# Two memory-recurrent attention layers with SwiGLU on one core: another TensorE order, and weight remainders loaded by 128-partition transfers

## The chip, the cores and the metric

One core of one Trainium2 chip runs the whole program. The metric is the device time of one execution in microseconds; the kernel before took 2661.49 us in the median of three runs (2657.86 to 2663.87). The engines are called PE (TensorE; PEld is its weight load), DVE (VectorE), ACT (ScalarE), POOL (GpSimd) and SP (SyncE, which only issues DMAs here).

## What is computed

The sequence has 2048 rows of 576 numbers. Two layers follow each other with the same weights; each is a recurrent attention over 64 segments of 32 rows, with 8 memory rows carried from segment to segment, and then a gated FFN of width 4608:

```python
for s in range(n_seg):                       # 64 segments, one after the other
    h = concat([mem, x[s]])                  # 8 + 32 rows
    q, k, v = h @ Wq, h @ Wk, h @ Wv         # 576 -> 32 heads x 128
    p = softmax(mask(q k^T * scale))         # 40 x 40 for each head
    o = (p @ v) @ Wo
    mem, out[s] = o[:8], o[8:]
# twice: x = x + A(layernorm(x)); x = x + B(layernorm(x))
# B: (silu(x @ w1) * (x @ w3)) @ w2
```

Weights and results are bfloat16.

## The kernel before

**Stages.** The two layers run interleaved: step t computes segment t of the first layer and segment t - 8 of the second (`LAG`), 72 steps in all. In steps 8 to 63 both layers are at work and share every matmul's columns (80 columns, 40 of each). Four steps make 128 rows, and their FFN runs spread over the next steps.

**The order of the work.** `make_nodes` builds a graph of work items with estimated durations (`dur`) and result latencies (`lat`), `plan` places them on the engines by these estimates, and the instructions are emitted in the planned order; each engine then runs its own list in order and waits by semaphores. DVE, ACT, POOL and the DMA list of SP get their order from the plan's estimated times and priorities. TensorE's order is not planned: it is a string of letters, `ORDER = FIRST + FOUR * 11 + LAST` (L222). FIRST covers steps 0 to 15, each FOUR four steps, LAST steps 60 to 71. One letter is one work item; the next item of that kind is taken. The kinds, with the matmuls of one and the mode of TensorE in which they run in FOUR:

- Q, q: queries and keys of four heads, 32 matmuls over the 512 even rows of the weights (full) and 8 over their last 64 rows (row)
- S: scores of a group of eight heads, 16 (col); P: weights times values, 8 or 16 (full or col); O, o: output projection, 32 (full) and 8 (col)
- V, v and G, g: values (V over four column strips, G full or col; v and g the last 64 rows)
- F, f: gate and up projection of 256 FFN columns (F full or col, f row); W, w: down projection of the two layers (full or col)
- n, a, b, p: transpositions of rows around the layer norms

A kind with two modes joins the mode that its neighbours have; when the mode changes, the matmuls in flight have to finish first, and the plan adds 0.1 to 0.14 us (L33, L34).

**The softmax of a group.** Behind S, DVE adds the mask and subtracts the maximum, ACT takes the exponential, DVE sums and writes the normalised probabilities to PB, SP issues a DMA transposition from PB to PTS (L1061), and P reads PTS. There are two buffers of PB and one of PTS (`POOLS`, L38): the transposition of a group waits until the P before it is done. The plan takes 1.27 us for the issue and 2.45 us until the data is there (L402). A step has four groups.

**Weights in the loop.** The FFN weights are read again for every four steps: a unit of 256 columns has four DMAs into one of two W13 buffers (two of the 512 even rows, two of the 64-row remainders) and one into one of two W2C buffers. They are issued by SP, on the same queue as the transpositions. A load waits until the unit before the last has been used up.

**Weights at the start.** Wq, Wk and Wv have 576 rows, four times 128 and a remainder of 64. T.W holds Wq in chunks 0 to 3, Wk in 4 to 7, and in chunk 8 both remainders: Wq's in partitions 0 to 63, Wk's in 64 to 127, all 4096 columns each. T.WV has Wv's remainder likewise: of each group of 1024 columns the first 512 in partitions 0 to 63, the others in 64 to 127. These are loaded by four DMAs of 64 partitions (`load_tails`, L701): SP issues Wq's and half of Wv's first of all, ACT issues Wk's, then x and the memory, then the rest of Wv's. Behind them SP issues sixteen pieces of 512 KB of Wq and Wk (first the left 2048 columns of both, then the right), then Wv, then Wo. `qk_tail` (L957) runs the two remainders of four heads as pairs of matmuls on opposite halves of the rows. At the end of the program chunk 8 and the rest of T.W take FFN weights (`tail_load`), 512 columns at a time, once the last step's q letters have read them.

Of the kernel before, what the change touches and what calls it, by code (L numbers as in the profile page):

```python
# [77 lines left out]
def plan(nodes, pools, letters):  # L78


    for n in nodes:
        for d in n.deps:
            d.outs.append(n)
    kinds = {}
    for n in nodes:
        if n.eng == "PE":
            kinds.setdefault(KINDS[n.name], []).append(n)
    its = {k: iter(v) for k, v in kinds.items()}
    seq = [next(its[c]) for c in letters]
    assert len(seq) == sum(len(v) for v in kinds.values())  # L90
    free = {k: [0.0] * c for k, c in pools.items()}
    t_eng = {e: 0.0 for e in ("PE", "ACT", "DVE", "POOL", "DMA", "SWD")}
    ready = {e: [] for e in t_eng}
    both = []
    mode, run = [], []
    order = []

    def settle():
        for x in run:
            x.mode = mode[0]  # L100
        run.clear()
    at = 0

    def push(n):
        if n.eng != "PE":
            (both if n.eng == "AD" else ready[n.eng]).append(n)

    def est(e, n):
        t = max(t_eng[e], n.ready)
        need = {}  # L110
        for s in n.acq:
            if s.i is None:
                need[s.pool] = need.get(s.pool, 0) + 1
        for p, c in need.items():
            t = max(t, sorted(free[p])[c - 1])
        return t

    for n in nodes:
        if n.left == 0:
            push(n)  # L120
    while len(order) < len(nodes):
        best = None
        for e in t_eng:
            if e == "PE":
                cands = seq[at:at + 1] if at < len(seq) and seq[at].left == 0 else []
            else:
                cands = ready[e] + (both if e in ("ACT", "DVE") else [])
            if not cands:
                continue
            ests = [(est(e, n), n) for n in cands]  # L130
            t = min(x for x, _ in ests)
            if t >= NOW:
                continue
            if best is None or t < best[0]:
                best = (t, e, ests)
        if best is None:
            raise RuntimeError(f"the plan is stuck at {at}: {seq[at].name}")
        t, e, ests = best
        st, n = min((x for x in ests if x[0] <= t + 1e-9), key=lambda x: x[1].prio)
        dur = n.dur  # L140
        if isinstance(dur, tuple):
            dur = dur[0] if e == "ACT" else dur[1]
        if e == "PE":
            at += 1
            if not any(m in mode for m in n.mode):
                dur += SWITCHES.get(f"{mode[0]} {n.mode[0]}", SWITCH) if mode else SWITCH
                settle()
                mode = n.mode
            mode = [m for m in mode if m in n.mode]
            run.append(n)  # L150
        elif n.eng == "AD":
            both.remove(n)
        else:
            ready[e].remove(n)
        n.start, n.end, n.by = st, st + dur, e
        t_eng[e] = n.end
        for s in n.acq:
            if s.i is not None:
                continue
            f = free[s.pool]  # L160
            s.i = min((i for i in range(len(f)) if f[i] <= st + 1e-9), key=lambda i: f[i])
            f[s.i] = NOW
        for s in n.rel:
            s.users -= 1
            s.end = max(s.end, n.end + (PE_LAT if e == "PE" else n.lat if e == "DMA" else EW_LAT))
            if s.users == 0:
                free[s.pool][s.i] = s.end
        for m in n.outs:
            m.ready = max(m.ready, n.end + (0.0 if m.eng == e == "PE" else n.lat))
            m.left -= 1  # L170
            if m.left == 0:
                push(m)
        order.append(n)
    settle()
    return order
# [20 lines left out]
def ewh(*ns):  # L196
# [11 lines left out]
    "oWQqfqqQQQfqSFSVvqqfQQFFPWSfqqQwQFSPaffOwWFPOFOPWOwfooooFfqqQQWQqqSQQqqSbQGgqqSQQgPGSGPGggOPOwOPoooOo"  # L208
)
FOUR = (  # L210
    "QqqqqQppQQVvSSnnQqfFQqfFSQQqfqPFOWoPSwFffOPFOowoWPFOoFfqfQQQQqqqwSWFSGfqgqQQQPQqgqWSSGFPFffggGGPwOOFPOOffWooooFv"
    "VqqqQQQwSFfqqqQQQSwWFSPFfqfqQQOwSPoWFFPffOOwPWOoooFfqqqQQWqSaQQQbSQqgqGSQPQqqgGOSPGggoOPGwOPooOo"
)
LAST = (
    "QqqqpQQQSnpQQqqqVvSnSQfqFFPqfQOWPSwoFffOPFoOFPwOffWooFQQQqqqFQSqffqFQQqgSWGSQPwQqqgfGSFPFgfgGwOPOGOPWOffooooFQQq"
# [16 lines left out]
def make_nodes(em, nseg, pools, o=Opt, dma_bw=230e3, load_bw=345e3):  # L232
# [122 lines left out]
    def step(t):  # L355
# [17 lines left out]
        for g in range(NG):  # L373
# [25 lines left out]
            pbs = node("DVE", w, em.sm_pb(t, g, sme, pb), deps=[d], prio=pf, acq=[pb], rel=[sme], name="pb")  # L399
            pts = Slot("pts")  # L400
            if nl == 2:
                tr = node("DMA", 1.27, em.ptr_dma(t, g, pb, pts), deps=[pbs], prio=pf - 0.02, acq=[pts], name="TR", lat=2.45)  # L402
            else:
                bt = banks()
                tr = node("PE", 8 * mm80, em.ptr(t, g, pb, bt), deps=[pbs], prio=pf + o.tr, mode="full/col", acq=[pts] + bt, name="TR")
# [54 lines left out]
    def job(j):  # L460
# [24 lines left out]
        def units(pps, at0, end):  # L485
            for at, pp in enumerate(pps, at0):
# [3 lines left out]
                for pr_ in (2 * pp, 2 * pp + 1):  # L490
                    prio = (s0 + 4 if end and not last else s0) + o.ff + (o.win if s0 + 4 < nst else o.last_win) * (2 * at + pr_ % 2) / NPR
                    if stays:
                        w13, w2 = kept[pr_]
                        ld = []
                        w2s.append(w2)
                    elif in_tail:
                        w13 = w2 = None
                        ld = tail[pp]
                    else:
                        keep = before_last and pp == npp - 1  # L500
                        w13, w2 = Slot("w13", users=2 + keep), Slot("w2", users=ne + keep)
                        kept[pr_] = w13, w2
                        ld = [node("DMA", kb(1152, 256) / dma_bw, em.load_w13(pr_, w13), prio=prio - 1, acq=[w13], lat=2.8, name="W13")]
                        lds.append(node("DMA", kb(256, 576) / dma_bw, em.load_w2(pr_, w2), prio=prio - 0.99, acq=[w2], lat=2.0, name="W2l"))
                        w2s.append(w2)
                    b = banks()
                    htt = Slot("htt", users=ne)
                    rel13 = [w13] if w13 else []
                    fm = node("PE", 16 * mm, em.ffn_up(ents, pr_, w13, b, in_tail, False), deps=wr + ld, prio=prio, mode="full/col",
                              acq=b + [htt], rel=rel13, name="FF")  # L510
                    ff = node("PE", 2 * mm, em.ffn_up(ents, pr_, w13, b, in_tail, True), deps=wr + ld, prio=prio + o.fft, mode="row",
                              acq=b + [htt], rel=rel13, name="FFt")
                    a = node("ACT", actc(256 * ne), em.ffn_tanh(ents, b, htt), deps=[fm, ff], prio=prio - 0.5, name="tanh")
                    c = node("DVE", 2 * dve(256 * ne) + 0.13, em.ffn_mul(ents, b, htt), deps=[a], prio=prio - 0.5, rel=b, name="mul")
                    last_up[:] = [fm, ff]
                    mids.append(c)
                    htts.append(htt)
# [24 lines left out]
        if last:  # L542
# [3 lines left out]
            for i in range(8):  # L546
                g = gates.get(i)
                tail.append([load("tail", kb(128, c), s0 + o.tail_at + 0.01 * i, em.tail_load(i, what, g), deps=dep + [g])
                             for what, c, dep in ((0, 9 * 512, qk_done[2 * i:2 * i + 2]), (1, 4 * 576, v_done))])
            shared.pop()()  # L550
        norm()
        if last:
# [55 lines left out]
class Emitter:  # L608
# [91 lines left out]

    def load_tails(self, what):  # L701
        def f(n):
            if what < 2:
                d, wd = (self.dma, self.a.wq) if what == 0 else (self.adma, self.a.wk)
                d(self.T.W[what * R64:(what + 1) * R64, 8, :], wd[4 * P:D, :])
            if what != 1:
                r = what // 2
                (self.adma if r else self.dma)(self.wv(True)[r * R64:(r + 1) * R64, :].rearrange("p (q n) -> p q n", q=NG),
                                               self.a.wv[4 * P:D, :].rearrange("p (q r n) -> r p q n", q=NG, r=2)[r])
        return f  # L710

    def wv(self, tail):
# [227 lines left out]
    def qk(self, t, u, b):  # L940
# [13 lines left out]
                                first and j == 0 and c == 0, c == 3)  # L954
        return f

    def qk_tail(self, t, u, b):  # L957
        def f(n):
            q0, q1 = self.qcols(t)
            HTt = self.ht(t)  # L960
            first = self.begin(b)
            for j in range(4):
                h0 = self.head(u // 2, 4 * (u % 2) + j) * E
                for kind in (0, 1):
                    rr = slice(kind * R64, (kind + 1) * R64)
                    self.mm(self.bk(b[kind])[:, j * SW:j * SW + q1 - q0], self.T.W[rr, 8, h0:h0 + E], HTt[rr, 4, q0:q1],
                            first and j == 0, True, tile_position=(kind * R64, 0))
        return f

    def qk_ev(self, t, u, r, q, b):  # L970
# [420 lines left out]
```

## Time and profile before

| what | us |
|---|---|
| three runs, median (lowest, highest) | 2661.49 (2657.86, 2663.87) |
| the profiled execution | 2662.86 |
| its span, from first to last instruction | 2661.1 |
| PE busy in 0 to 56, 56 to 528 | 26.8, 456.8 |
| PE busy in 528 to 2222 (eleven times FOUR) | 1678.4 |
| PE busy in 2222 to 2600, 2600 to 2661 | 369.8, 53.5 |

The loads at the start, by the trace of the DMA issues (issue to landing, us from the start of the span): Wk's remainder 0.7 to 5.5, Wq's 0.7 to 7.9, x 1.3 to 8.4, half of Wv's remainder 1.4 to 9.7 and the other half 2.8 to 13.7; the first 512 KB of Wq 2.3 to 11.5, the eighth piece landed at 21.2, the sixteenth at 34.7, Wv between 37.2 and 44.7, Wo between 47.6 and 56.7.

In a row of the profile, the numbers behind the bar of a group are busy time, mean duration and idle time before; a timeline row has the start, the time taken, the engine, line, operation and tiles, and in brackets the idle time before it with what ended it. A row of the stretches has the stretch, its length, busy time and instructions of PE, PEld, DVE, ACT and POOL, the granted TensorE clock, the busy share of the DMA engines and GB/s. The granted clock over the span is 0.994.

### The profile page before, as it was taken

The numbers are of one execution on the slowest core, as the hardware profiler recorded it, in microseconds if no ns is written. First come the engines' busy times: TensorE is split into PE (matmuls) and PEld (weight loads), VectorE is DVE, ScalarE is ACT, GpSimd is POOL, SyncE is SP. The second block draws the span as 40 slices with busy tenths as digits, with TensorE's granted clock in tenths as the row PEclk, the third lists the DMA queues.
The fourth block names the chain that finished last, engine by engine and source line by source line (L and its number), as shares of the span: only waits on it lengthen the run. The fifth ranks groups of instructions, "written<-read, shape, count | busy, mean of one in ns | idle before, by whom it ended". The sixth has DMA issues, their size and how long they took to land.

```text
span 2661.1 us, 134392 instructions
## 1 busy us (share of the span) xinstructions
PE 2585.4 (97%) x59795; PEld 2228.9 (84%) x59795; DVE 2025.0 (76%) x5276; ACT 1252.0 (47%) x3612; POOL 337.1 (13%) x399
## 2 busy tenths in 40 slices
PE   5999999999999999999999999999999999999998
PEld 4788888888888888888888888888888888888887
DVE  4787777787787778777777777777778777777876
ACT  2555453454445444444544444454544445454453
POOL 1111110110111011011101101110111111011110
PEclk8999999999999999999999999999999999999999
DMA  9064845556565556555554655645465564544457
GB/s 321 4 179 123 189 105 149 127 136 148 128 144 105 147 125 145 142 131 147 113 139 116 162 128 141 154 110 136 113 155 125 143 157 101 129 119 128 128 158 236
DMA packets 688135, 371.55 MB, mean 140 GB/s; under 512 B 234072, under 2 KB 682336, under 8 KB 686912
## 3 DMA queue, kind: packets, MB, share of 16 engines
q1 hardware_dynamic: 684016, 355.07, 53.2%
q8 instruction: 467, 7.65, 1.2%
q0 software_dynamic: 3024, 6.93, 0.9%
q10 hardware_dynamic: 512, 0.94, 0.1%
q14 instruction: 116, 0.95, 0.1%
HBM read 306.72 MB, written 2.36 MB: 116 GB/s over the span
## 4 chain that ended last, share of the span: by engine, by line
PE 67%; DMA 7%; DVE 4%; ACT 1%; SPq 1%; issue 1%; POOL 0%; DVEq 0%; POOLq 0%; ACTq 0%
PE bank L632 67%; DMA PTS<-PB 4%; DMA W<-in_B_w_dram 2%; DVE STAT L638 1%; DMA W2C<-in_B_w_dram 1%; DVE SME L638 1%; SPq L641 1%; DVE PB L638 1%; DVE V L638 1%; ACT V L635 0%; DVE XR L638 0%; DVE HTT L638 0%; DVE QKT L638 0%; POOL PB L1052 0%; ACT QKT L635 0%
## 5 line engine op out<-in xcount | busy, mean ns | idle before, releaser
L632 PEld LDWEIGHTS <-W 128*128 128x128 bf16 (+2 forms) x32576 | 1270.4, 101 | 137.4 <-issue 58.6
L632 PE MATMUL bank<-HT,W 128*128 128x80 bf16 (+3 forms) x23040 | 800.0, 197 | 25.9 <-DMA W<-in_A_Wk_dram 8.5
L632 PE MATMUL bank<-XTB,W 128*64 128x256 bf16 (+5 forms) x9536 | 663.2, 263 | 6.3 <-DMA W<-in_B_w_dram 5.9
L1052 POOL MEMSET PB<- 128x1024 bf16 x288 | 273.9, 951 | 1958.6 <-DMA PTS<-PB 1292.0
L635 ACT ACTIVATE QKT<-bank 128x256 bf16<-128x256 f32 (+4 forms) x1456 | 338.9, 310 | 284.6 <-PE bank L632 272.1
L632 PE MATMUL bank<-OT,WO 128*128 128x80 bf16 (+3 forms) x11520 | 417.3, 198 | 1.5 <-issue 0.8
L632 PEld LDWEIGHTS <-WO 128*128 128x128 bf16 (+1 forms) x11520 | 386.2, 102 | 36.8 <-issue 20.9
L635 ACT ACTIVATE V<-bank 64x512 bf16<-64x512 f32 (+1 forms) x625 | 351.7, 585 | 120.2 <-PE bank L632 112.3
L632 PE MATMUL bank<-WV,HT 128*32 128x512 bf16 (+4 forms) x3688 | 370.2, 384 | 1.3 <-DVE HT L638 0.7
L632 PE MATMUL bank<-W2C,HTT 128*64 128x288 bf16 (+1 forms) x3296 | 321.5, 287 | 4.7 <-DMA W2C<-in_B_w_dram 4.7
L635 ACT ACTIVATE OT<-bank 128x320 bf16<-128x320 f32 (+1 forms) x384 | 144.3, 403 | 335.6 <-PE bank L632 332.1
L638 DVE TENSOR_REDUCE STAT<-SME 104x8 f32<-104x320 f32 (+1 forms) x576 | 274.6, 477 | 32.4 <-ACT SME L635 27.0
L638 DVE TENSOR_TENSOR PB<-SME,STAT 40x128 bf16<-40x128 f32 (+4 forms) x912 | 275.5, 336 | 12.2 <-POOL PB L1052 0.4
L638 DVE SCALAR_TENSOR_TENSOR HTT<-HTT,bank 128x512 bf16<-128x512 bf16 (+1 forms) x324 | 201.2, 621 | 105.0 <-ACT HTT L635 101.9
L632 PEld LDWEIGHTS <-HT 128*32 128x32 bf16 (+4 forms) x3688 | 159.0, 100 | 133.3 <-issue 29.7
L632 PEld LDWEIGHTS <-HTT 128*64 128x64 bf16 (+1 forms) x3376 | 230.2, 106 | 42.0 <-issue 8.4
L635 ACT ACTIVATE HTT<-bank 128x512 bf16<-128x512 f32 (+1 forms) x324 | 174.2, 550 | 189.2 <-PE bank L632 187.7
L638 DVE SCALAR_TENSOR_TENSOR XR<-bank,XR 128x288 f32<-128x288 f32 x574 | 242.4, 446 | 18.0 <-PE bank L632 14.9
L635 ACT ACTIVATE SME<-SME 104x320 f32<-104x320 f32 (+1 forms) x288 | 135.2, 469 | 208.1 <-DVE SME L638 205.6
L638 DVE CAST QKT<-bank 128x128 bf16<-128x128 f32 (+2 forms) x592 | 158.2, 315 | 94.5 <-PE bank L632 92.6
L638 DVE TENSOR_TENSOR HTT<-HTT,bank 128x512 bf16<-128x512 bf16 (+1 forms) x324 | 203.5, 628 | 32.5 <-DVE HTT L638 1.4
L638 DVE CAST V<-bank 32x512 bf16<-32x512 f32 (+1 forms) x239 | 163.4, 684 | 33.6 <-PE bank L632 29.4
(59 smaller groups left out, 1414.6 us busy)
## 6 DMA issues: line engine op xcount, KB each, us to landing
W<-in_B_w_dram SPq DMA_DIRECT2D x608, 256.0 KB, 3.9
W2C<-in_B_w_dram SPq DMA_DIRECT2D x304, 288.0 KB, 3.7
W<-in_B_w_dram SPq DMA_DIRECT2D x608, 32.0 KB, 3.8
W<-in_B_w_dram SPq DMA_DIRECT2D x16, 512.0 KB, 8.6
W<-in_A_Wq_dram SPq DMA_DIRECT2D x9, 512.0 KB, 10.2
WO<-in_A_Wo_dram SPq DMA_DIRECT2D x4, 1152.0 KB, 16.7
XR<-in_A_x_dram POOLq DMA_DIRECT2D x16, 288.0 KB, 4.0
WV<-in_B_w_dram SPq DMA_DIRECT2D x8, 576.0 KB, 7.1
```

What stands on the lines that cost most here:

```text
L632: self.ch("PE", self.nc.tensor.matmul(out, lhsT=lhsT, rhs=rhs, start=start, stop=stop, skip_group_check=True, **k))
L635: self.ch("ACT", self.nc.scalar.activation(*a, **k))
L638: self.ch("DVE", getattr(self.nc.vector, fn_)(*a, **k))
L641: self.ch("SP", self.nc.sync.dma_start(out=out, in_=in_))
L1052: return lambda n: self.ch("POOL", self.nc.gpsimd.memset(self.T.PB[:, pb.i], 0.0))
```

## The change

FOUR gets another order of the same letters. Three latencies of the plan become shorter: the transposition's from 2.45 to 2.0 us, the W13 load's from 2.8 to 2.0, and a slot that a DMA gives back counts as free earlier (only the last stores do that). FIRST and LAST keep their strings. DVE, ACT and SP are planned anew with these numbers.

The remainders get another place and other transfers. A helper `pair` loads 2n columns of 64 rows as two halves of n columns, the left half into partitions 0 to 63, the right one into 64 to 127, with one DMA whose source pattern is `h p n` (2 x 64 x n). Wq's go by two such pairs (n = 1024) and Wv's by four (n = 512, two on each queue); the middle half of Wk goes by one pair, and its first and last quarter by a 64-partition transfer each. `qk_tail_at` gives rows and columns of a head's remainder, and the tail loads at the end name the q letters that read a block.

```diff
-            s.end = max(s.end, n.end + (PE_LAT if e == "PE" else n.lat if e == "DMA" else EW_LAT))
+            s.end = max(s.end, n.end + (PE_LAT if e == "PE" else EW_LAT))
...
 FOUR = (
-    "QqqqqQppQQVvSSnnQqfFQqfFSQQqfqPFOWoPSwFffOPFOowoWPFOoFfqfQQQQqqqwSWFSGfqgqQQQPQqgqWSSGFPFffggGGPwOOFPOOffWooooFv"
-    "VqqqQQQwSFfqqqQQQSwWFSPFfqfqQQOwSPoWFFPffOOwPWOoooFfqqqQQWqSaQQQbSQqgqGSQPQqqgGOSPGggoOPGwOPooOo"
+    "QQppQqqqqQvVSnnSQFqqfqqQQFSqffQPFwOSPWFoffPOFOWwPFOoooFfqfqQQQQqqSWGSFqqfgQQQPQgqqwSGSFPGffggFWGPOwOFPOOoooowVqfq"
+    "vQQQQqfqWSFSFfqqqQQwWQFPfqfSFwQOPSWFoFPffOOWPwOoooFqqfQQWQSqqqQQaSbQQqgqqGSQgPGSGPGggOPOwOPoooOo"
 )
...
-                tr = node("DMA", 1.27, em.ptr_dma(t, g, pb, pts), deps=[pbs], prio=pf - 0.02, acq=[pts], name="TR", lat=2.45)
+                tr = node("DMA", 1.27, em.ptr_dma(t, g, pb, pts), deps=[pbs], prio=pf - 0.02, acq=[pts], name="TR", lat=2.0)
...
-                        ld = [node("DMA", kb(1152, 256) / dma_bw, em.load_w13(pr_, w13), prio=prio - 1, acq=[w13], lat=2.8, name="W13")]
+                        ld = [node("DMA", kb(1152, 256) / dma_bw, em.load_w13(pr_, w13), prio=prio - 1, acq=[w13], lat=2.0, name="W13")]
...
-                             for what, c, dep in ((0, 9 * 512, qk_done[2 * i:2 * i + 2]), (1, 4 * 576, v_done))])
+                             for what, c, dep in ((0, 9 * 512, qk_done[2 * i:2 * i + 1] + [me[f"QKt{u}"] for u in range(8) if any(em.qk_tail_at(k, u)[1] == 512 * i for k in (0, 1))]), (1, 4 * 576, v_done))])
...
     def load_tails(self, what):
         def f(n):
-            if what < 2:
-                d, wd = (self.dma, self.a.wq) if what == 0 else (self.adma, self.a.wk)
-                d(self.T.W[what * R64:(what + 1) * R64, 8, :], wd[4 * P:D, :])
+            def pair(d, out, wd, at, n):
+                d(out, wd[4 * P:D, at:at + 2 * n].rearrange("p (h n) -> h p n", h=2))
+
+            if what == 0:
+                for i in (0, 1):
+                    pair(self.dma, self.T.W[:, 8, i * 1024:(i + 1) * 1024], self.a.wq, i * 2048, 1024)
+            elif what == 1:
+                self.adma(self.T.W[R64:P, 8, 3072:4096], self.a.wk[4 * P:D, 0:1024])
+                pair(self.adma, self.T.W[:, 8, 2048:3072], self.a.wk, 1024, 1024)
+                self.adma(self.T.W[0:R64, 8, 3072:4096], self.a.wk[4 * P:D, 3072:4096])
             if what != 1:
-                r = what // 2
-                (self.adma if r else self.dma)(self.wv(True)[r * R64:(r + 1) * R64, :].rearrange("p (q n) -> p q n", q=NG),
-                                               self.a.wv[4 * P:D, :].rearrange("p (q r n) -> r p q n", q=NG, r=2)[r])
+                for q in range(what, what + 2):
+                    pair(self.adma if what else self.dma, self.wv(True)[:, q * 512:(q + 1) * 512], self.a.wv, q * 1024, 512)
...
+    def qk_tail_at(self, kind, u):
+
+        i = u // 2
+        block = (3 if i in (0, 3) else 2) if kind else i // 2
+        return R64 * (i % 2 ^ kind), block * 1024 + u % 2 * 512
+
     def qk_tail(self, t, u, b):
...
             for j in range(4):
-                h0 = self.head(u // 2, 4 * (u % 2) + j) * E
                 for kind in (0, 1):
-                    rr = slice(kind * R64, (kind + 1) * R64)
-                    self.mm(self.bk(b[kind])[:, j * SW:j * SW + q1 - q0], self.T.W[rr, 8, h0:h0 + E], HTt[rr, 4, q0:q1],
-                            first and j == 0, True, tile_position=(kind * R64, 0))
+                    r0, w0 = self.qk_tail_at(kind, u)
+                    rr = slice(r0, r0 + R64)
+                    self.mm(self.bk(b[kind])[:, j * SW:j * SW + q1 - q0], self.T.W[rr, 8, w0 + j * E:w0 + (j + 1) * E], HTt[rr, 4, q0:q1],
+                            first and j == 0, True, tile_position=(r0, 0))
```

More of the change, by code (lines that the diff above doesn't have):

```diff
@@ L210 @@
 FOUR = (
-    "QqqqqQppQQVvSSnnQqfFQqfFSQQqfqPFOWoPSwFffOPFOowoWPFOoFfqfQQQQqqqwSWFSGfqgqQQQPQqgqWSSGFPFffggGGPwOOFPOOffWooooFv"
-    "VqqqQQQwSFfqqqQQQSwWFSPFfqfqQQOwSPoWFFPffOOwPWOoooFfqqqQQWqSaQQQbSQqgqGSQPQqqgGOSPGggoOPGwOPooOo"
+    "QQppQqqqqQvVSnnSQFqqfqQQFSqffQPFwOSPWFoffPOFOWwPFOoooFfqfqQQQQqqSWGSFqqfgQQQPQgqqwSGSFPGffggFWGPOwOFPOOoooowVqfq"
+    "vQQQQqfqWSFSFfqqqQQwWQFPfqfSFwQOPSWFoFPffOOWPwOoooFqqfQQWQSqqqQQaSbQQqgqqGSQgPGSGPGggOPOwOPoooOo"
 )
```

## The prediction

> **What bounds the kernel now.** I read the shares of the engines first, then the busy time and DMA rate stretch by stretch, then TensorE's waits by stage, then its timeline, then the transposition tile and the DMA queues.
>
> ```profile
> PE 2585.4 (97%) x59795; PEld 2228.9 (84%) x59795; DVE 2025.0 (76%) x5276; ACT 1252.0 (47%) x3612; POOL 337.1 (13%) x399
> q1 hardware_dynamic: 684016, 355.07, 53.2%
> q10 hardware_dynamic: 512, 0.94, 0.1%
> ```
>
> TensorE is busy for 97% of the span. Of the idle 76 us, 29.2 lie in the first 56 us (busy there 26.81) and 15.6 in 528 to 2222 us, where the eleven repeats of FOUR run. Those are the two places the change touches. In the repeats TensorE's waits are these:
>
> ```profile
> PE bank L632 <- DMA PTS<-PB: 7.0, 14, 1.0
> PE bank L632 <- ACT HT L635: 3.8, 11, 0.3
> PE bank L632 <- DMA W2C<-in_B_w_dram: 3.6, 6, 1.3
> PE bank L632 <- DMA W<-in_B_w_dram: 1.2, 3, 0.8
> ```
>
> So the order is nearly without holes, and what holes there are belong to transpositions and weight loads. At the start the loads decide. The rows of the stretches end in clock, DMA share and GB/s; the timeline shows single matmuls, each behind one 512 KB piece:
>
> ```profile
> 4.00:5.00 1.00, 0.00 (x0) 0.00 (x0) 0.84 (x3) 0.00 (x0) 0.90 (x3) 1.00 0.76 172
> 6.00:7.00 1.00, 0.00 (x0) 0.00 (x0) 0.89 (x3) 0.00 (x0) 0.00 (x0) 1.00 0.75 144
> 15.00:16.00 1.00, 0.07 (x1) 0.00 (x0) 0.00 (x0) 0.00 (x0) 0.00 (x0) 1.00 1.02 406
> ...
> 16.13 0.22 PE L632 MATMUL bank<-HT,W 128*128 128x40 bf16 x1 [1.06 <-DMA W<-in_A_Wq_dram]
> 17.41 0.22 PE L632 MATMUL bank<-HT,W 128*128 128x40 bf16 x1 [1.06 <-DMA W<-in_A_Wk_dram]
> ...
> 21.24 3.51 PE L632 MATMUL bank<-HT,W 128*128 128x40 bf16 x97 [1.05 <-DMA W<-in_A_Wk_dram]
> ```
>
> A piece comes every 1.276 us, 411 GB/s over 16 engines, 25.7 GB/s for one. While the 64-row remainders move (2 to 9 us) the seven rows add to 1574 KB, 225 GB/s on average. TensorE first runs through at 21.24 us, and the same stream holds it again until 34.8 us.
>
> **Term 1, fewer changes of TensorE's mode.** A change costs some 0.1 us: from the start of a WO to the next letter's start is 1.15 us without one and 1.24 with one, of a Q 1.15 and 1.24, of an F 1.75 and 1.85. Counted by the letters' modes (P, F, W, w, G and p join either full or col), one pass through FOUR has 65 changes before and 59 after. Adding the trace's price of every letter (Q 1.15, q 0.146, S 0.22, P 0.29, O 1.15, o 0.15, F 1.75, f 0.22, W and w 0.98, G 1.74, V 1.74) and of every change gives 152.2 us a pass before and 151.6 after: **-0.57, times 11 = -6.3 us**. The measured passes before average 154.0, so 1.9 of each is waiting.
>
> **Term 2, transpositions nearer to their users.** There is one PTS buffer: a transposition is issued only when the PV before it is done. In groups bound by that, the issue stands 0.53 us behind the start of that PV. The landing comes later:
>
> ```profile
> DMA to landing us min/median/max: 2.9/3.0/5.8
> ```
>
> So a P can follow the P before it by 0.53 + 2.9 + 0.05 = 3.5 us at best. Of the 154 transpositions of the repeats whose landing shows, half land within 3.03 us, a quarter take over 4.15 (behind weight loads on the same queue), a tenth over 4.54. The planner's constants (1.27 + 2.45 before, 1.27 + 2.0 after) lie above the best and below the slow quarter. Letter sums between P and P, before to after: the first step's third group 5.07 to 3.85 (P W F o f f P), the last step's second 5.34 to 3.99 (P G S G P), third 4.11 to 3.84 (P G g g O P), fourth 4.16 to 3.57 (P O w O P: 0.29 + 1.15 + 0.98 + 1.15); the others keep 4.2 or more. Laying the 154 landings over these distances, the mean waiting of a pass is 1.09 us before (I read some 1.2 at P in the trace) and 2.00 after; with each place's own landings, 0.84 and 1.53. **+0.8, times 11 = +9 us.** Bounds: landings all below the median give +0.1 a pass, twice as many slow ones +1.6.
>
> **Term 3, weight loads nearer too.** W13 has two buffers, so unit k+2 can be loaded when unit k's F and f are through. For the third unit of the pass this distance falls from 6.33 to 5.11 us (its f stands first, and that needs the last of four loads); before, its load landed 4.2 to 6.2 us after the release, 5.1 in the median: mean waiting 0.4 us after, none before. The W2C distances fall at worst from 6.6 to 5.9. Another unit loses 1.3 of 8.2 us where SP's queue is itself held by a transposition; if that holding stays, 1.1 us more, if not, nothing. **+0.4, times 11 = +4.5 us** (bounds 0 and +18).
>
> Some places must win (one W2C wait of 0.2 us a pass stood where the new order has 0.3 us more room), so I take terms 2 and 3 together at +13, and terms 1 to 3 at **+7 us** (bounds -6 and +18).
>
> **Term 4, the remainders on few engines.** Queue q10 is ACT's, and its 512 packets can be counted out: 64 rows of Wk, 128 of x, 8 of the memory, 256 of Wv make 456, and 56 are left, which is 16 + 16 + 16 + 8: one closing packet for each engine used, and 8 for the transfer with 8 rows. So the number of engines follows a pattern's outermost count. The new pairs read `h p n`, outermost count 2. If both sides must be divisible, each runs on two engines, the same two.
>
> The Trainium skill states this outright (DMA: Bandwidth & Descriptors, "Why a DMA increments its semaphore by 16 and not by 1"): the slowest dimension of both patterns decides, by the largest count up to 16 that divides both. The eight closing packets agree; no run shows an outermost 2 yet.
>
> Price: Wq's 512 KB, half of Wk's (256 KB) and Wv's 512 KB go by pairs, 1,310,720 B, 655,360 for each of the two engines: 25.5 us at 25.7 GB/s. From the other side, q1's mean packet takes 0.532 x 16 x 2661.1 / 684016 = 33 ns for 519 B, a 4096 B row 159 ns (eight in 1.276 us); the line through both gives 87 ns for 2048 B and 51 for 1024 B, and 192 + 256 such rows take 29.8 us. The eight 512 KB pieces of the first half then still take 8 x 1.276 = 10.2 us of these two engines, and SP issues them behind the pairs. Starting at 2.2 us, with 1 us for x and the rest, all of it is there at 39 to 43 us instead of 21.2. The stream has pauses of 1.8 and 1.5 us later (pieces at 24.3 and 29.6 us) that the two late engines can fill. x lands later as well (it shares the two engines), but the 2.4 us of normalisation behind it are then still over before the weights are there. Behind the stream stand the second half, Wv and Wo; TensorE waits for them in turn until some 52 us and cannot catch up, being busy afterwards. I take **+17 us** (bounds +12 and +22).
>
> **Edits that I cost at nothing.** The remainder's new columns: a q has the same eight matmuls on opposite row halves. The order of DVE, ACT and SP in FIRST and LAST, replanned with the shorter constants: TensorE waits for transpositions 3.1 us in 56 to 528 and 2.5 after 2222, so the bound is 3 us either way. The last step's tail loads wait for other q letters: these run in one row within 1.3 us (2594.98), and SP sits idle from 2599.7 to 2609.9 behind the WO gate; without that cover, 1.3 us. The slot's end after a store touches the last stores only: nothing comes behind.
>
> **Sum.** -6.3 + 13.3 + 17 = +24. The profiled execution took 2662.9 us, its span 2661.1 and 1.8 around it; 2662.9 + 24 = 2687. It lies 1.4 over the median 2661.5, so I predict **2686 us**.
>
> **The rivals.** (a) *The pairs do spread over 16 engines and both halves of the partitions*: then 1574 KB move in 3.8 us instead of 7, -3.2, and with +7 of the order 2665. For it: rows of 64 partitions cost half the rate and pairs would mend just that. Against: the eight closing packets. (b) *As (a), and the new order waits no more than the old*, because the landings are mostly at 2.9 to 3.0 us and 3.57 just holds them: -6.3 - 3.2 gives **2652**, faster. The place is the last step's four PVs and the f of the third unit; it decides once the added waiting is below 0.6 us a pass. For it: only a quarter of the landings is slow, and the fourth PV's landing was never over 3.25. Against: the second and third PV of that step had landings over 4.2 us in five of nineteen readable cases. (c) *Two engines, but an order that wins its 6 us*: 2661.5 + 17 - 6 = 2672. (d) *SP stands still behind the pairs*: each puts 64 rows on one engine's ring, and SP cannot issue the next pieces until they drain; with the slow rows and all of term 3, 2661.5 + 22 + 18 = 2702.
>
> **How the numbers follow.** The forecast, with its own range 2674 to 2700, has 0.52; (c) 0.16, (d) 0.05, (a) 0.14, (b) 0.13. The range of eight in ten must hold (a) and (c), so it goes from 2658 to 2702. About 0.2%, 5.3 us, is what the measurement can tell from no change: faster 0.14, same 0.13 (mostly (a)), slower 0.73.
>
> **What would show it.** Term 4: the first run of matmuls on whole 128-row pieces starting near 39 us, a DMA rate of 50 to 150 GB/s from 5 to 20 us, and q10 with fewer closing packets. Near 18 us it would be (a), and the forecast fails by 20 us. Term 1: passes whose quickest stretch is 0.6 us shorter. Terms 2 and 3: TensorE's waits for PTS in the repeats near 15 us instead of 7.0, at the last step's PVs above all, and a wait for W of W13 before the pass's third f. If passes average under 153.5 us, the order was a gain and I mis-sized the landings.

## The result, and the profile after

| | us |
|---|---|
| before, median of four runs (lowest, highest) | 2660.84 (2657.86, 2663.87) |
| changed, median of four runs (lowest, highest) | 2678.89 (2674.57, 2684.02) |
| ratio, with its 95% interval | 1.0071 [1.0059, 1.0083] |
| profiled execution, before and changed | 2662.86 and 2679.74 |
| its span | 2661.1 and 2678.0 |

The changed kernel is slower, by 16 to 22 us. The prediction was 2686: the direction and the main cause came as foretold, the size was 7 us too large.

The shares of the engines and the DMA queues of the changed kernel (busy time, share of the span, instructions; packets, MB, share of 16 engines):

```profile
PE 2576.1 (96%) x58915; PEld 2225.2 (83%) x58915; DVE 2041.2 (76%) x5253; ACT 1226.9 (46%) x3635; POOL 335.0 (13%) x399
q1 hardware_dynamic: 684184, 355.07, 53.6%
q10 hardware_dynamic: 710, 0.94, 0.1%
```

TensorE is busy for 9.3 us less than before and issues 880 matmuls fewer, 80 for each repeat of FOUR, and yet the span is 16.9 us longer: more of it is waiting. The queue q10 moves the same 0.94 MB in 710 packets instead of 512. 64 rows of Wk, 128 of the half that goes by the pair, 64 of Wk, 128 of x, 8 of the memory and 256 of Wv make 648; the 62 left are 16 + 2 + 16 + 16 + 8 + 2 + 2. **Each pair closes with two packets**, so each ran on two engines. SP's queue q1 agrees: its remainders now have 512 rows instead of 320, and with two closing packets for each of four pairs instead of 16 for each of two transfers that makes 168 packets more, which is what the two pages differ by (684184 and 684016).

The stretches of the start (stretch, length, busy time and instructions of PE, PEld, DVE, ACT, POOL, granted clock, DMA share, GB/s):

```profile
6.00:8.00 2.00, 0.00 (x0) 0.00 (x0) 1.78 (x5) 0.00 (x0) 0.00 (x0) 1.00 0.13 49
...
12.00:14.00 2.00, 0.00 (x0) 0.00 (x0) 0.00 (x0) 0.00 (x0) 0.00 (x0) 1.00 0.16 55
18.00:20.00 2.00, 0.00 (x0) 0.00 (x0) 0.88 (x3) 0.00 (x0) 0.00 (x0) 1.00 0.13 49
40.00:42.00 2.00, 0.42 (x2) 0.21 (x2) 0.00 (x0) 0.00 (x0) 0.00 (x0) 1.00 1.02 412
```

From 6 us to 22 us two of sixteen engines work (a DMA share of 0.13 to 0.16), at some 25 GB/s each; at 40 us the 512 KB pieces move at the old 412 GB/s. SP's issues and TensorE's first work show what that delays (start, time taken, engine, line, operation and tiles, and in brackets the idle time before it with what ended it):

```profile
0.75 1.41 SPq L641 DMA_DIRECT2D W<-in_A_Wq_dram  x2
2.20 15.19 SPq L641 DMA_DIRECT2D WV<-in_A_Wv_dram  x2
17.43 14.45 SPq L641 DMA_DIRECT2D W<-in_A_Wq_dram  x4
```

```profile
21.57 0.75 PE L632 MATMUL bank<-ident,XN 128*64 128x128 bf16 x10 [21.57 <-DVE XN L638]
...
33.22 0.22 PE L632 MATMUL bank<-HT,W 128*128 128x40 bf16 x1 [8.72 <-DMA W<-in_A_Wq_dram]
...
42.77 3.51 PE L632 MATMUL bank<-HT,W 128*128 128x40 bf16 x97 [1.18 <-DMA W<-in_A_Wk_dram]
```

SP needs 15.19 us to issue two pairs of Wv. The three pairs issued ahead of them (Wq's two and Wk's, 786 KB) take 15.7 us at 50 GB/s, which fits two engines that take entries no faster than they move the data; no view names what an issue waits for, so this is argued. Only at 17.43 does SP come to the first whole 512 KB piece (at 2.3 before), and from 6 to 22 us the other fourteen engines have next to nothing to do. The first run of 97 matmuls starts at 42.77 us instead of 21.24, which is +21.5.

Part of that comes back. The row in which the second half of Wq and Wk has arrived, and the rows some 20 us on, after (first fence) and before (second):

```profile
52.95 1.02 PE L632 MATMUL bank<-HT,W 128*128 128x40 bf16 x25 [1.04 <-DMA W<-in_A_Wk_dram]
73.79 0.56 PE L632 MATMUL bank<-PTS,V 128*64 128x40 bf16 x16
75.73 2.39 PE L632 MATMUL bank<-OT,WO 128*128 128x40 bf16 x80 [1.38 <-issue]
83.97 1.25 PE L632 MATMUL bank<-HT,W 128*128 128x40 bf16 x32
```

```profile
34.79 1.02 PE L632 MATMUL bank<-HT,W 128*128 128x40 bf16 x25 [1.06 <-DMA W<-in_A_Wk_dram]
55.35 0.56 PE L632 MATMUL bank<-PTS,V 128*64 128x40 bf16 x16
55.85 2.23 PE L632 MATMUL bank<-OT,WO 128*128 128x40 bf16 x80
62.77 0.97 PE L632 MATMUL bank<-HT,W 128*128 128x40 bf16 x32
```

Row by row the lag is 18.2, 18.4, 19.9 and 21.2 us. The pauses in the old stream of loads give back 3.4 us of the 21.5. Then 1.4 us are lost in front of an output projection, in a gap whose releaser the trace doesn't name (the run with the remainders alone, below, has it too, 1.43 us), and 1.3 more in a stretch in which the same 32 matmuls take 1.25 us instead of 0.97: the granted clock is 0.50 there, and was 1.00 before. The repeats start 20.9 us late.

TensorE's waits in the eleven repeats of the changed kernel (total us, times, longest):

```profile
PE bank L632 <- DMA PTS<-PB: 14.9, 27, 1.5
PE bank L632 <- ACT HT L635: 3.4, 10, 0.3
PE bank L632 <- DMA W<-in_B_w_dram: 2.2, 2, 1.1
PE bank L632 <- DMA W2C<-in_B_w_dram: 0.6, 2, 0.3
```

Waiting for transpositions has doubled, from 7.0 to 14.9; waiting for weights (W and W2C) has fallen from 4.8 to 2.8. The eleven repeats take 1695.4 us instead of 1694.1. So the account of the profiled executions is +20.9 before the repeats, +1.3 in them and -5.3 in LAST, together +16.9.

### The profile page after: what moved, and what is told of

It is laid out like the page before. It is cut to its first block, busy times and chain, and to the rows that moved or that the text cites. A ratio compares the mean times of both kernels' runs of the same rounds, so it can differ in the third digit from the quotient of the medians.

```text
span 2678.0 us, 132815 instructions
## 1 busy us (share of the span) xinstructions
PE 2576.1 (96%) x58915; PEld 2225.2 (83%) x58915; DVE 2041.2 (76%) x5253; ACT 1226.9 (46%) x3635; POOL 335.0 (13%) x399
## 3 DMA queue, kind: packets, MB, share of 16 engines
q1 hardware_dynamic: 684184, 355.07, 53.6%
## 4 chain that ended last, share of the span: by engine, by line
PE 80%; DMA 12%; DVE 3%; SPq 2%; issue 1%; ACT 1%; POOL 1%; DVEq 0%; POOLq 0%; ACTq 0%
PE bank L632 80%; DMA PTS<-PB 8%; SPq L641 2%; DMA W<-in_B_w_dram 2%; DMA W2C<-in_B_w_dram 1%; DVE V L638 1%; DMA W<-in_A_Wk_dram 1%; DVE STAT L638 1%; POOL PB L1064 1%; DMA W<-in_A_Wq_dram 1%; DVE SME L638 1%; DVE PB L638 0%; DVE HTT L638 0%; ACT V L635 0%; SPq L1073 0%
## 5 line engine op out<-in xcount | busy, mean ns | idle before, releaser
L632 PEld LDWEIGHTS <-W 128*128 128x128 bf16 (+2 forms) x31872 | 1255.4, 100 | 153.5 <-issue 68.1
L635 ACT ACTIVATE QKT<-bank 128x256 bf16<-128x256 f32 (+4 forms) x1546 | 356.7, 314 | 310.0 <-PE bank L632 299.1
L635 ACT ACTIVATE V<-bank 64x512 bf16<-64x512 f32 (+1 forms) x583 | 329.1, 584 | 127.2 <-PE bank L632 120.3
L632 PE MATMUL bank<-WV,HT 128*32 128x512 bf16 (+3 forms) x3952 | 373.4, 383 | 1.3 <-DVE HT L638 0.7
L638 DVE TENSOR_REDUCE STAT<-SME 104x8 f32<-104x320 f32 (+1 forms) x576 | 273.3, 474 | 15.7 <-ACT SME L635 9.6
L632 PEld LDWEIGHTS <-HT 128*32 128x32 bf16 (+3 forms) x3952 | 167.4, 101 | 115.2 <-issue 19.5
L638 DVE CAST V<-bank 64x512 bf16<-64x512 f32 (+1 forms) x281 | 192.2, 685 | 40.5 <-PE bank L632 34.1
L638 DVE CAST QKT<-bank 128x192 bf16<-128x192 f32 (+2 forms) x502 | 135.8, 314 | 86.0 <-PE bank L632 84.6
```

The lines of the kernel that those rows point to most:

```text
L632: self.ch("PE", self.nc.tensor.matmul(out, lhsT=lhsT, rhs=rhs, start=start, stop=stop, skip_group_check=True, **k))
L635: self.ch("ACT", self.nc.scalar.activation(*a, **k))
L638: self.ch("DVE", getattr(self.nc.vector, fn_)(*a, **k))
```

## The experiments

Each edit is given against the changed kernel or the kernel before, as said. Ratios are against runs of the kernel before on the same chip; its median was 2659.96 us beside the first four experiments and 2662.03 beside the others.

**The two halves of the change, each alone.** The first is the changed kernel with order, latencies and slot rule of before, so only the remainders are new:

```diff
 FOUR = (
-    "QQppQqqqqQvVSnnSQFqqfqQQFSqffQPFwOSPWFoffPOFOWw...
+    "QqqqqQppQQVvSSnnQqfFQqfFSQQqfqPFOWoPSwFffOPFOow...
...
-    ... name="TR", lat=2.0)
+    ... name="TR", lat=2.45)
...
-    ... lat=2.0, name="W13")]
+    ... lat=2.8, name="W13")]
```

> The new remainders with the old order and the old latencies. Theory (pairs run on two engines): the start is that of the changed kernel, first full run of matmuls near 42.8 us and +19 to +22 us at 250 us, so 2679 to 2683 us, the whole loss. Rival (the loss belongs to the order or to the new plan): the start late, but made up later, under 2672.

The second is the kernel before with the new FOUR, the two latencies of 2.0 and the new slot rule; the remainders are loaded and used as before.

> The new order and latencies with the old remainders; the start is that of the kernel before. Theory (the new waits of the repeats eat what the saved mode changes bring, and LAST, planned anew, wins some 4 us): 2655 to 2661 us. Rival (the prediction's sum of terms 1 to 3, +7): 2666 to 2670. Second rival (the gain seen in LAST was chance of one profile): 2661 to 2665.

| | median us | ratio |
|---|---|---|
| remainders alone | 2679.32 | 1.0071 [1.0056, 1.0085] |
| order alone | 2661.26 | 1.0000 [0.9991, 1.0009] |

The remainders carry the whole loss (+15 to +23 us), and the order is worth nothing that shows, within 2.4 us either way. Its 2661.26 us lies between the theory's range and the second rival's; LAST is taken up again at the end of this section. TensorE's waits in the repeats, of the remainders alone and then of the order alone, say that the halves don't mix:

```profile
PE bank L632 <- DMA PTS<-PB: 7.0, 14, 1.0
PE bank L632 <- ACT HT L635: 3.4, 10, 0.3
PE bank L632 <- DMA W2C<-in_B_w_dram: 2.2, 5, 0.8
```

```profile
PE bank L632 <- DMA PTS<-PB: 15.8, 27, 1.5
PE bank L632 <- ACT HT L635: 3.8, 11, 0.3
...
PE bank L632 <- DMA W<-in_B_w_dram: 1.4, 3, 0.7
PE bank L632 <- DMA W2C<-in_B_w_dram: 0.7, 2, 0.5
```

With the old order the waits for transpositions are the old 7.0 us, with the new one 15.8, whatever the start does.

**Is it the two engines?** The changed kernel, with the same bytes to the same places, but each pair as two transfers of 64 partitions:

```diff
             def pair(d, out, wd, at, n):
-                d(out, wd[4 * P:D, at:at + 2 * n].rearrange("p (h n) -> h p n", h=2))
+                for h in (0, 1):
+                    d(out[h * R64:(h + 1) * R64], wd[4 * P:D, at + h * n:at + (h + 1) * n])
```

> The changed kernel with each pair as two transfers of 64 partitions, so that the outermost count is 64 instead of 2; places, rows, bytes and queues stay, seven more issues. Theory (two engines): the rate between 6 and 20 us rises from 50 to over 200 GB/s, first full run near 20 to 23 us, 2655 to 2661 us. Rival (short rows, or scattered places of the rows): the same rows stay, so 2676 or more.

A smaller dose splits the pairs of Wv alone (n = 512), and leaves Wq's and Wk's as pairs:

> The changed kernel with only the four pairs of Wv split in two; Wq and Wk keep three pairs, 384 KB on each of two engines instead of 640. Theory (two engines, 25.7 GB/s each): 10.2 us less than the changed kernel, 2667 to 2671 us, first full run near 32.5. Rival (a fixed price for any pair, or only the last one counts): within 3 us of the changed kernel or of the one with all pairs split.

| | median us | ratio | first run of 97 matmuls at |
|---|---|---|---|
| changed | 2678.89 | 1.0071 [1.0059, 1.0083] | 42.77 |
| Wv's pairs split | 2674.51 | 1.0051 [1.0038, 1.0064] | 35.50 |
| all pairs split | 2665.05 | 1.0019 [1.0009, 1.0029] | 22.70 |
| before | 2660.84 | 1 | 21.24 |

The start follows the dose, and with no pair left it lies 1.5 us behind the old one. Both times missed what the theory foretold, though: 2665.05 us against 2655 to 2661, and 2674.51 against 2667 to 2671. The queue's packets of the version with all pairs split, its start stretches and SP's issues:

```profile
q10 hardware_dynamic: 800, 0.94, 0.1%
```

```profile
2.00:4.00 2.00, 0.00 (x0) 0.00 (x0) 1.69 (x1) 0.00 (x0) 1.95 (x4) 1.00 0.86 240
6.00:8.00 2.00, 0.00 (x0) 0.00 (x0) 1.78 (x5) 0.00 (x0) 0.00 (x0) 1.00 0.98 194
8.00:10.00 2.00, 0.00 (x0) 0.00 (x0) 1.64 (x5) 0.00 (x0) 0.00 (x0) 1.00 0.63 131
```

```profile
3.78 4.25 SPq L641 DMA_DIRECT2D WV<-in_A_Wv_dram  x4
8.25 2.37 SPq L641 DMA_DIRECT2D W<-in_A_Wq_dram  x4
```

800 packets are the 648 rows, nine transfers closing with 16 and one with 8. SP reaches the first whole piece at 8.25 us instead of 17.43, and the rate from 6 to 8 us is about four times that of the pairs (194 against 49 GB/s). It was not better than the old start, though: 131 GB/s at 8 to 10 us, where the kernel before has 267. Of the 5.1 us by which its median stays behind the kernel before (2659.96 us beside it), the start explains 1.5; the other 3.6 are not settled. Splitting Wv alone moved the start by 7.3 us, not by 10.2, and the median by only 4.4. Matmul by matmul, the lead of its profile over that of the changed kernel is 7.3 us at the start, 5.0 at 157 us, and anything from 2 to 7 us later on; what took the rest is open too.

**Would both halves of the partitions at once be faster?** That was what rival (a) needed. Every pair's lower half goes from SP's queue and its upper half from ACT's, as 64-partition transfers side by side:

```diff
-                    pair(self.dma, self.T.W[:, 8, i * 1024:(i + 1) * 1024], self.a.wq, i * 2048, 1024)
+                    half(d, h, self.T.W[:, 8, i * 1024:(i + 1) * 1024], self.a.wq, i * 2048, 1024)
...
+                    for q in range(4):
+                        half(lo, 0, self.wv(True)[:, q * 512:(q + 1) * 512], self.a.wv, q * 1024, 512)
+            else:
+                for q in range(4):
+                    half(hi, 1, self.wv(True)[:, q * 512:(q + 1) * 512], self.a.wv, q * 1024, 512)
```

> The changed kernel with every pair as two transfers of 64 partitions, the lower half from SP and the upper half from ACT, so that both are in flight together. Theory (64 partitions take half the rate, two halves at once the whole): over 300 GB/s from 3 to 8 us, first full run near 19 to 20 us instead of 22.9 with the pairs split on one queue, 2658 to 2662 us. Rival (two halves share one rate anyway, or x comes too late): first full run at 22 us or later, 2663 to 2667.

It measured 2664.95 us, 1.0013 [1.0001, 1.0025], with the first run of matmuls at 22.35. Two of its stretches:

```profile
4.00:6.00 2.00, 0.00 (x0) 0.00 (x0) 1.73 (x5) 0.00 (x0) 1.72 (x5) 1.00 1.02 277
8.00:10.00 2.00, 0.00 (x0) 0.00 (x0) 1.48 (x5) 0.00 (x0) 0.29 (x1) 1.00 0.81 168
```

213, 277, 192 and 168 GB/s in the four stretches from 2 to 10 us are no more than the 274, 217, 184 and 267 of the kernel before. So rival (a)'s gain of 3.2 us was not to be had in this way.

**What makes the order wait?** The kernel before with the new FOUR and nothing else, so with the old latencies:

> The new order of TensorE with the old latencies in the plan and the old remainders. Theory (the string alone sets the waits; the latencies only shift the plan's books): within 3 us of the run with the new latencies, 2658 to 2664 us, waits at P of 2.0 to 2.5 us a pass. Rival (the shorter latencies order SP and DVE in a way that makes or spares waits): 5 us or more apart.

2662.49 us, 1.0000 [0.9989, 1.0012]. The waits in front of the P letters were 1.89 us a pass (just under the range foretold) against 2.47 in the run with the new latencies; single profiles of the new order scatter from 1.89 to 2.47, so the string sets them and the latencies have no effect that shows.

The largest single wait of the new order stands at the first step's third group, P W F o f f P, 0.66 us a pass. The order-alone version with one O brought in front of that P (the next O moves behind, the letters stay the same):

```diff
-    "...QPFwOSPWFoffPOFOWwPFOooo...
+    "...QPFwOSPWFoffOPFOWwPFOooo...
```

> The new order and latencies with the old remainders, and one P of FOUR put behind the next O (PWFoffPOF becomes PWFoffOPF), so that the first step's third P stands 5.0 instead of 3.85 us behind the P before it, with as many mode changes. Theory (the new waits are the single PTS buffer's, P after P): the wait of 0.66 us a pass at this place goes, little comes elsewhere, 0.4 to 0.7 us a pass, 2653 to 2657 us, a version below the kernel before. Rival (the wait is for something else, or only moves on to the next P): 2660 to 2663.

2658.97 us, 0.9993 [0.9981, 1.0005]: no difference from the kernel before that can be told. Its waits in the repeats:

```profile
PE bank L632 <- DMA PTS<-PB: 14.4, 20, 2.3
...
PE bank L632 <- DMA W2C<-in_B_w_dram: 3.0, 4, 1.5
```

At the P that was moved, waiting fell from 0.66 to some 0.1 us a pass. At the next P it rose from 0.09 to 0.41, and at the last W of the pass that stands in front of a Q, where the W2C load is awaited, from 0.10 to 0.35. Few waits make these rises: at the next P mainly three of the eleven passes, one with the 2.3 us of the first row, and at the W the four waits of the second. With one PTS buffer each transposition starts from the P before it, so a P that comes later can make the next one late; that the wait moved on in this way is argued from one profile, not shown. A second PTS buffer would cut this chain; that was not tried.

**The kernel before, once more**, for the scatter of a single profile:

> The kernel before, profiled once more. Theory (the 5 us that LAST lost between 2222 and 2661 us in the first profile against all later ones were chance of that execution): LAST takes 433 to 436 us here too. Rival (the replanned orders or the tail loads made LAST quicker): 438 to 440 us again.

One run, 2666.76 us. LAST took 435.8 us in it, 439.1 in the first profile of the same kernel, and 433.2 to 437.7 in the profiles of all the others. So of the 5.3 us that LAST seemed to win, 3.3 were the first profile's slow LAST, and the rest lies within the scatter of the others; no effect of the change on LAST shows.

## Why the prediction was right, and where its size was off

The idle time and the waits by order, worked out from the traces (us for each pass through FOUR; passes, three profiles with the old order and six with the new one):

| | old order | new order | predicted change |
|---|---|---|---|
| pass without its waits | 152.1 | 151.3 | -0.57 |
| waits in front of P | 1.07 to 1.23 | 1.89 to 2.47 | +0.8 |
| all other waits, mean | 0.74 | 0.67 | +0.4 |
| eleven passes | 1691.0 to 1696.0 | 1690.8 to 1696.5 | +7 |

The split into work and waiting hangs on how a wait is counted. By the profile's own idle gaps of TensorE, which are shorter, a pass without them takes 152.6 us with the old order and 152.0 with the new one, and the gaps are 1.4 and 2.1 us a pass, of which 0.7 and 1.5 in front of P.

**Term 4 (predicted +17, bounds 12 and 22).** Right in cause and nearly in size. Two engines, 49 to 55 GB/s, a first run of matmuls at 42.77 inside the 39 to 43 foretold, two closing packets for each pair. The Trainium skill's rule (DMA: Bandwidth & Descriptors, "Why a DMA increments its semaphore by 16 and not by 1") is shown here for an outermost 2, where before only the eight closing packets spoke for it. The mechanism of rival (d) was at work in this: SP did stand still behind the pairs, which may be why the start lies at the upper end. Its price didn't stay, since the pauses of 1.8 and 1.5 us gave back 3.4 us, as the working had it; at 74 us the lag was 18.4. What the sum lacked are the 2.8 us lost behind that, at the gap and at the half clock. Measured alone, the remainders cost 19.4 us by the medians, 2.4 above the forecast. So this error and that of the other terms, which were too large, partly cancel: that the total is only 7 us off is in part luck.

**Terms 1 to 3 (predicted +7, measured about 0).** This is where the 7 us too many come from, and the step is "**+0.4, times 11 = +4.5 us**" of term 3, with the size of term 1 if one goes by the table. There term 1 was mis-sized to the safe side: a pass without its waits became 0.85 us shorter, not 0.57, which is -9.4 us in eleven passes. By the idle gaps it became 0.6 us shorter, as foretold. Term 2 was right: the waits in front of P rose by 1.0 us a pass in the table and by 0.7 in the idle gaps (+0.8 foretold), to 14.9 us in the changed kernel (15 foretold). It erred in the place, though: the last step's P's, named first, wait 0.53 us a pass, the first step's third group alone 0.66, where the distance is 3.85 us and the transposition, issued among weight loads, lands after 4.04 in the median of the profile with the order alone (4.46 in that of all six). Term 3 failed outright, by either count. No wait for W13 grew in front of the third f; the other waits fell by 0.07 us a pass. The working took the release of a W13 buffer to be one moment, that at which both F and f are through. The four loads wait for their own rows each, and the rows of F come free earlier: the first of them is issued 1.0 us before the f that I reckoned with has ended, and the third f starts 6.0 us after this issue. The last of the four lands 4.4 to 6.1 us after it in the six profiles with the new order, so the room goes from 1.8 us down to none, and no pass has a wait there. So -9.4 + 11 - 0.8 is about +1, and the repeats by the trace have +1.3; by the idle gaps it is -6.6 + 8.1 - 0.8.

**The edits costed at nothing.** The remainders' new columns, the latencies and the slot rule show no cost: remainders alone lose what the start loses, and order alone loses nothing. FIRST and LAST differ by up to 6 us between profiles of one kind, so a bound of 3 us either way could not be read more closely.

**The rivals.** (a) and (b) needed pairs over 16 engines and fell with the rate at 6 us. (c), two engines with an order that wins its 6 us, was as near in time as the forecast (2672 against 2679) and wrong in the order, which wins its matmul time and loses it again at P. (d) named a delay that was there and a total that was not.

## What to carry to other kernels

Before a load's pattern is reshaped to fill all 128 partitions, look at its outermost count: a 2 in front means two engines for the whole transfer, and here the queue of 512 KB pieces stood behind it for 15 us. Two plain transfers of 64 partitions in its place took back 14 us; closing packets on the queue and a DMA share of 0.13 are the signs to look for. An order that saves mode changes by moving a consumer nearer to its DMA wins only what the buffer's chain allows: with a single buffer the 0.6 to 0.85 us saved in a pass came back as 0.7 to 0.9 us of waiting, and moving one consumer brought no gain that shows.

## What was not expected of the hardware

**DMA issues of SP and ACT wait for each other's landings at the start.** In the version with all pairs split, from the ninth on, an issue begins 0.01 to 0.02 us after an earlier transfer of the two queues has landed: 3.78 after 3.77, 4.95 after 4.94, 6.60 after 6.58, 7.57 after 7.55. The kernel before does the same (5.49 after 5.475, 7.94 after 7.92). So eight transfers are in flight at most. The trace also shows what does it: the two engines use eight completion semaphores in turn (100 and 102 to 108), and from the ninth on each issue first waits for the semaphore that it will count up itself. So the limit is in the program, and no limit of the chip is shown by it. That it is this which kept the split version from beating the old start (131 GB/s at 8 to 10 us) is argued, not shown.

**Half clock outlasts the idle time.** Every kernel has stretches at a granted clock of 0.50 in its first 200 us; summed as length times (1 - clock), 8.5 us with the remainders alone, 11.9 before, 13.7 changed, 20.5 with Wv's pairs split. The time lost is less than this sum even where TensorE decides: the 32 matmuls above took 1.25 us at 0.50 and 0.97 at 1.00. Here are two rows of the changed kernel, and the rows of before for the same work:

```profile
78.00:82.00 4.00, 2.78 (x84) 2.60 (x82) 0.50 (x3) 0.68 (x3) 0.00 (x0) 0.50 0.78 212
82.00:86.00 4.00, 4.00 (x118) 3.32 (x112) 2.32 (x6) 1.61 (x6) 0.00 (x0) 0.50 0.03 8
```

```profile
58.00:62.00 4.00, 2.86 (x119) 2.71 (x114) 1.05 (x5) 1.17 (x5) 0.00 (x0) 1.00 1.05 284
62.00:66.00 4.00, 3.52 (x111) 2.75 (x108) 2.30 (x6) 1.27 (x4) 0.00 (x0) 1.00 0.05 16
```

TensorE is busy without a gap from 81.1 us, and its clock comes back only between 87 and 88. The Trainium skill (TensorE: Matmul & The Clock Gate, "Part 1: The HAM clock gate (the "warmup" mystery)") gives about 3.4 us of sustained work for that, in windows that run freely and don't start with the work. This trace has about 6 us and agrees: its clock changes only at multiples of 3.41 us (here at 77.17 and 87.41), and 84.0 to 87.41 is the first of these three windows that TensorE fills without a gap. What set the half clock here, after an idle time of 1.4 us at most in the 8 us before it, is open.
